# A gated FNet block on one core: one matrix of y's second stage made in chunk 1, then one weight per chunk; two first y units in a row; x of the third block added by accumulating DMA

## The chip, the core and the metric

The kernel runs on one core of a Trainium2 chip. The metric is the device time of one execution in microseconds. For the kernel before there are three timed executions (685.96, 687.7 and 689.08 us, median 687.7) and one profiled execution (683.77 us).

The engines named below: PE (TensorE) multiplies matrices, DVE (VectorE) adds and multiplies element by element, ACT (ScalarE) copies, scales and applies functions, POOL (GpSimd) here only issues DMAs, SP (SyncE) issues most of the DMAs.

## The reference

```python
def _A_ref(x, dft_seq_re, dft_seq_im, dft_hid_re, dft_hid_im):
    a = jnp.einsum("bsd,ed->bse", x, dft_hid_re)
    b = jnp.einsum("bsd,ed->bse", x, dft_hid_im)
    y = jnp.einsum("ts,bse->bte", dft_seq_re, a) - jnp.einsum("ts,bse->bte", dft_seq_im, b)
    return y

def _B_ref(x, w1, b1, w2, b2):
    h = jnp.einsum("bsd,df->bsf", x, w1) + b1
    zero = jnp.zeros_like(h)
    r = jnp.where(h > zero, h, zero)
    h = r * r
    out = jnp.einsum("bsf,fd->bsd", h, w2) + b2
    return out

x = A_x                                # [1, 2048, 512], fp32
xn = _layernorm(x, axis=-1)
s = _A_ref(xn, ...)                    # the DFT over hidden and sequence, real part
g = _silu(_B_ref(xn, ...))             # D = 512, F = 1792
return x + s * g
```

## The kernel before

**Numbers.** All matrix products are fp32 products made of three passes over operands split in two: a high part HI, rounded to the fast type by ACT (`split_hi`, line 130), and the remainder LO, subtracted by DVE (`split_lo`, line 133). `split` makes both, so DVE's half waits for ACT's. Most products of 2x2 blocks are done with seven block products instead of eight (`PRODUCTS`, numbers 1 to 7). Each needs sums of blocks of its operands ahead of the split, on DVE: three instructions per operand, 128x512, 128x256 and 128x256 (`sums_b`, lines 273 to 275, and `sums_a`, lines 279 to 285). The sums of the results are on DVE too (`combine`, line 322, in the chunks; lines 731 and 734 in the units).

**Stages.** The program is one long order written out by hand: the order of the Python calls is the order of the instructions on each engine, and each engine works its own list from front to back.

1. *Chunks* (to about 335 us). The sequence DFT, applied first, in eight chunks of 256 columns over the layer-normalised tokens. Chunks 0 and 1 use eight products with moving operands of 512 columns (`one_product`, line 356). Chunks 2 to 7 use seven products (`mm`, line 341), in eight steps j = 0 to 7 each; a step is 7 x 6 = 42 matmuls of 256 columns. Step n's operand `g` comes from a tile `u` that SP loads four steps ahead (`step_load`), that DVE sums two steps ahead (`step_sums`) and that ACT and DVE split one step ahead (`step_split`). At the end of a chunk the seven results are combined by eight operations: three at the end of the chunk's last step, four behind step 0 of the next, one behind step 1, which then stores the chunk (`PQD`).
2. *The weights beside it.* Between the steps, weights of later stages are prepared by generators, which `go(name)` carries on by one piece: `d0` to `d3` are the hidden DFT's four matrices (the second stage of y), `v0`, `v1`, `v6` three of the seven slices of w1. Each has four pieces (`weight`): a load, the three sums, and two splits (128x768 and 128x1024), each with a store of the result to DRAM. `y0` to `y2` prepare the first operands of the y stage (load, sums, two splits), `p0` to `p3` load the `d` matrices back, half a matrix a piece. The table `EARLY` says which piece runs behind which step (chunk, j) of chunks 2 to 7; `d0` and `d1` are made in chunks 0 and 1 by other means.
3. *y units* (to about 391 us). Eight units `YUnit`, each seven products of 12 matmuls of 256 columns (`products`, line 721). The products of a unit collect in four regions: A (products 1, 2), B (6, 5, 3), C (4), D (7). A is copied, negated, into B by ACT as its start value (`seed`, line 140), B into C likewise. DVE makes C22 from B (line 731) after product 5, and C21 from C (line 734) after product 4; ACT copies A, B and D out, and stores the unit (line 760). Unit 0 runs its products in a row (1, 7, 6, 2, 5, 4, 3). From unit 1 on, the units overlap: a unit's first product runs ahead of the last three of the unit before. The operands of a unit are two tiles `yraw` (load, sums, split).
4. *H units* (to about 543 us). 28 units `HUnit` for the first matrix of the FFN (7 slices of F by 4 blocks of 512 tokens), pipelined in the same way, their outputs stored to DRAM. `H_SIDE` says which pieces of other work run in three places of each unit: `V2` to `V5` make the remaining slices of w1, `w0` to `w6` the slices of w2, `x` the tokens, `h` the operands of the last stage.
5. *Output* (to the end). Four blocks of 512 tokens by seven slices, `outer`, line 827, matmuls into `m_o` (blocks 1 to 3) and `m_last` (block 4); operands `hr` are loaded, summed and split ahead (`h` pieces, and the table `O_SIDE`). A block is finished while the next one runs: `finish` applies silu on ACT, multiplies by y (`times`, line 877, DVE) and adds x. It adds x either by DVE (`plus`, line 882, which then stores on SP) or by a DMA that POOL issues and that adds into the tile in SBUF (`add_x`, line 865), in which case a later `put` (line 868) stores on SP. How many tiles `load_fin` loads decides which: with four all parts are added by DVE, with three the first two by DVE and the others by DMA. Before, it loads three for the first two blocks and four for the third (`c > NTC - 3`).

Of the kernel before, what the change touches and what calls it, by code (L numbers as in the profile page):

```python
# [35 lines left out]


EARLY = {
# [7 lines left out]
}  # L46
# [13 lines left out]

H_SIDE = {
    0: ((), ("V2", "x2"), ("x3",)),
    1: (("V4",), ("V3",), ("V5", "k6")),
    2: ((), ("V4", "V5"), ("k6",)),
    3: ((), ("V5",), ("w4",)),
    4: ((), ("x2", "x3", "m2"), ("x4",)),
# [16 lines left out]
    23: ((), ("h1",), ("w3",)),  # L83
    24: ((), ("w1", "w2"), ("w6", "h2")),
    25: ((), ("w2", "w3"), ("h3", "l4")),
    26: ((), ("w3", "w6"), ("l5",)),
    27: ((), ("h2",), ()),
}
ACT_PAIR = (7, 10, 13, 15, 17, 18, 19, 20, 26)
O_SIDE = {0: (("h4",), ("h5",)), 1: ((), ("w6",))}  # L90

EPS = 1e-5
HI, LO = 0, 1
# [31 lines left out]
def fnet_gated_kernel(ctx, tc, x, xt, ct, wd, w1, w2, b1, b2, out):  # L125
# [41 lines left out]
    def operand_buf(tag, name, step, shape=(2, 7, 256)):  # L167

        first = START.get(tag, 0)
        skip = (step - first) % 4 * LANE  # L170
        size = shape[0] * shape[1] * shape[2]
        room = ROOM.get(tag, 0)
        flat = buf(tag, [P, size + (room or skip)], name, F32R)
        a, b, c = shape
        return flat[:, skip:skip + size].rearrange("p (a b c) -> p a b c", a=a, b=b, c=c)
# [234 lines left out]
        if n < 2 * NC:  # L410
            sums_rows(yraw[n], yraw[n][:, 4:8], True)

    def y_split(n):
        if n < 2 * NC:
            g = yop[n] = operand_buf(Y_HOME[n // 2 % 3][n % 2], f"yg{n}", 1)
            split(g[:, HI], g[:, LO], yraw[n][:, 0:7])

    def y_early(n):

# [109 lines left out]
    for k in range(2):  # L529
        nc.sync.dma_start(PQD[0][:, k].rearrange("p k n -> p (k n)"), plain[k])  # L530
    for j in range(NJ - 1):
        split(*plain_parts(1, j + 1))
        load_c(*order[NJ + j + 4])
        if j == 1:
            go("d0", "d1")
        for h in range(2):
            products(1, j, h)
        beside(split_s1(j - 1) if j else 0)
    step_sums(0)
    step_split(0)  # L540
    step_load(3)
    split_s1(NJ - 2)
# [296 lines left out]
    def load_fin(c):  # L839

        if c < NTC - 1:
            ts = [buf(f"pq{n // 2}{n % 2}", [P, 2, 512], f"fin{c}_{n}") for n in range(4 if c > NTC - 3 else 3)]
        else:
            t = buf("xc5", [P, 3, 2, 512], f"fin{c}")
            ts = [t[:, n] for n in range(3)] + [buf("pq10", [P, 2, 512], f"fin{c}_3")]
        fin[c] = ts
        for n, t in enumerate(ts):
            src = (Y[c], x[c * TC:(c + 1) * TC])[n // 2]
            for i in range(2):
                nc.sync.dma_start(t[:, i].rearrange("p (k e) -> p k e", k=2), at(src, 2 * (n % 2) + i))  # L850
# [32 lines left out]
        nc.sync.dma_start(at(out[c * TC:(c + 1) * TC], k)[:, cols], z.rearrange("p (k e) -> p k e", e=256))  # L883

    go("m0")
    unit = YUnit(0)
    some(closing, 5)
    nc.sync.dma_start(PQD[NC - 1].rearrange("p h k n -> p (h k n)"), e)
    unit.products(1)
    unit.seed("B", "A")  # L890
    y_sums(3)
    unit.products(7)
    unit.m7()
    unit.products(6)
    unit.seed("C", "B")
    y_split(3)
    y_load(6)
    unit.products(2)
    unit.c11()
    unit.products(5)  # L900
    unit.c22()
    unit.products(4)
    unit.c21()
    unit.products(3)
    unit.c12()
    y_sums(4)
    y_sums(5)
    before = None
    for u in range(1, NC):
        n = 2 * u + 2  # L910
        unit = YUnit(u)
        y_split(n)
        y_load(n + 3)
        unit.products(1)
        unit.seed("B", "A")
        if before:
            before.c11()
            before.products(5)
            before.c22()
# [73 lines left out]
    for n in range(NTC * NP):  # L993
        c, p = divmod(n, NP)
        last = c == NTC - 1
        if n and not last and p == 0:

            ms = Banks(c)
            for k in (2, 4, 5):
                bias(ms[k], k)  # L1000
        elif last and p == 0:

            ms = {k: bank(t, f"m{k}_last") for k, t in
                  {1: "b20", 2: "b21", 6: "b30", 7: "b31", 5: "bb", 3: "ba"}.items()}
# [12 lines left out]

        go(*O_SIDE.get(n, ((), ()))[0])
        if n == 1:
            for k, i in ((1, 1), (2, 1), (6, 1), (4, 1), (5, 0), (3, 0), (7, 1), (5, 1), (3, 1)):  # L1020
                add(k, i)
        elif n and (not last or p < REST):
            for k in ORDER if p else FIRST_LAST if last else FIRST:
                add(k, p)
        if n == 1:

            nc.scalar.activation(stats[:, 0, 0, 0:1], stats[:, 0, 0, 0:1], AF.Silu)
        if not n:
            go("h2")
        go(f"h{n + 3}")  # L1030
        if p == NP - 1 and not last:
            e = buf("e", [P, 4, 512], f"z{c}")
            list(combine(lambda k: halves(e[:, k]), ms))
            done_next = c, e
        if c and not last and p in (3, 4):
            put(*done, p - 1)
        go(*[f"h{n + 2}"][:n], *O_SIDE.get(n, ((), ()))[1], f"h{n + 6}")
        if p == (3 if last else 5):
            load_fin(c)
        if p == NP - 1 and not last:  # L1040
            done = done_next
        elif c:
            for k in ((2, 3), (0,), (1,), (), (), (), ())[p] if not last else ((), (0,), (1,), (2,), (3,), (), ())[p]:
                finish(*done, k)


    e = buf("u", [P, 4, 512], f"z{c}")
# [88 lines left out]
```

## Time and profile before

| | us |
|---|---|
| timed runs, median (lowest, highest) | 687.7 (685.96, 689.08) |
| the profiled execution, its own time | 683.77 |
| its span (first to last event of the profile) | 682.0 |
| busy in it: PE | 672.8 |
| DVE | 605.2 |
| ACT | 357.4 |
| POOL | 6.4 |
| mean granted TensorE clock | 0.998 |

How to read the rows below. A row of groups names the line, the engine, the operation, out<-in with the tiles' names, the shape, the count, then busy time and mean. In the timeline a row begins with start and busy time in us, and in brackets stands the engine's idle time before it and what released it. In the chain of waits (what ended last, followed back), a row is start, time, engine, tile and line, with the count of instructions in a row. In the windows, the columns are the window, its length, then the busy time of PE (with the count), of PE's weight loads, the granted clock, the share of DMA and its GB/s. A matmul's end is modelled, so PE's rows can touch although PE loses a little between them.

### The profile page before, as it was taken

What the parts mean: (1) busy time and instruction counts of PE and PEld (TensorE: products, weight loads), DVE (VectorE), ACT (ScalarE), POOL (GpSimd) and SP (SyncE); (2) the same over time, 40 slices, a digit from 0 to 9 for tenths busy, and PEclk for the clock granted to TensorE, in tenths of its full rate; (3) what the DMA queues carried; (4) which work ended last, traced back from release to release, by engine and by line L of the source; (5) the groups of instructions that cost most, each with busy time, mean ns of one, the idle gap of its engine ahead of it and who ended that gap; (6) DMA issues with size and microseconds to landing.
All of it is one profiled execution on the core that took longest, in us unless ns stands there. A gap on an engine that the chain in (4) does not pass through costs nothing.

```text
span 682.0 us, 13144 instructions
## 1 busy us (share of the span) xinstructions
PE 672.8 (99%) x5440; PEld 648.9 (95%) x5440; DVE 605.2 (89%) x849; ACT 357.4 (52%) x475; POOL 6.4 (1%) x9
## 2 busy tenths in 40 slices
PE   9999999999999999999999999999999999999996
PEld 6778789999999999999999999999999999999996
DVE  7999969999999898798899979999847879999996
ACT  4445645444444343435364557787878765454451
POOL 0000000000000000000000000000000000101000
PEclk9999999999999999999999999999999999999999
DMA  8625656758587764349468657679445956777745
GB/s 295 212 93 216 209 232 220 270 182 289 177 281 260 265 231 159 120 162 361 155 234 287 223 186 276 215 283 325 154 155 181 373 191 212 187 218 200 241 147 171
DMA packets 51723, 150.82 MB, mean 221 GB/s; under 512 B 4944, under 2 KB 19536, under 8 KB 50256
## 3 DMA queue, kind: packets, MB, share of 16 engines
q1 hardware_dynamic: 44096, 129.80, 55.8%
q10 hardware_dynamic: 6208, 18.88, 7.0%
q0 software_dynamic: 1360, 1.31, 1.5%
q8 instruction: 42, 0.69, 0.4%
q14 instruction: 17, 0.14, 0.1%
HBM read 101.98 MB, written 47.99 MB: 220 GB/s over the span
## 4 chain that ended last, share of the span: by engine, by line
PE 75%; DVE 18%; issue 3%; ACT 2%; DMA 1%; ACTq 0%; DVEq 0%
PE m L341 22%; PE m_o L827 14%; PE r_B L721 12%; PE pq_b L356 8%; PE r_A L721 8%; DVE g L133 5%; PE r_C L721 4%; PE r_D L721 3%; DVE c L322 3%; PE pq_ba L356 2%; PE pq_bb L356 1%; PE pq_bc L356 1%; ACT g L130 1%; DMA u<-in_ct 1%; DVE u L273 1%
## 5 line engine op out<-in xcount | busy, mean ns | idle before, releaser
L341 PE MATMUL m<-g,xc 128*128 128x256 f32 x2016 | 231.7, 277 | 1.3 <-DVE g L133 1.0
L341 PEld LDWEIGHTS m<-g,xc 128*128 128x128 f32 x2016 | 230.7, 188 | 2.3 <-DVE g L133 2.3
L130 ACT ACTIVATE g<-u 128x1792 fp32r<-128x1792 f32 (+3 forms) x70 | 100.0, 1428 | 139.9 <-PE m L341 91.1
L133 DVE TENSOR_TENSOR g<-u,g 128x1792 fp32r<-128x1792 f32 (+3 forms) x70 | 117.5, 1679 | 19.1 <-ACT g L130 18.8
L827 PE MATMUL m_o<-w,g 128*128 128x256 f32 x882 | 100.5, 276 | 0.0
L827 PEld LDWEIGHTS m_o<-w,g 128*128 128x128 f32 x882 | 100.3, 188 | 0.0
L130 ACT ACTIVATE g<-hr 128x1792 fp32r<-128x1792 f32 (+2 forms) x31 | 48.2, 1565 | 43.0 <-DVE hr L285 17.7
L721 PE MATMUL r_B<-xT,w 128*128 128x256 f32 x504 | 67.6, 277 | 0.3 <-DVE h L791 0.2
L356 PE MATMUL pq_b<-g,xc 128*128 128x512 f32 x240 | 66.2, 394 | 0.3 <-ACT xc L130 0.2
L721 PEld LDWEIGHTS r_B<-xT,w 128*128 128x128 f32 x504 | 61.8, 188 | 1.1 <-DVE h L791 0.7
L133 DVE TENSOR_TENSOR g<-hr,g 128x1792 fp32r<-128x1792 f32 (+2 forms) x31 | 56.7, 1839 | 5.1 <-ACT g L130 5.1
L356 PEld LDWEIGHTS pq_b<-g,xc 128*128 128x128 f32 x240 | 43.7, 188 | 13.0 <-ACT xc L130 3.0
L721 PE MATMUL r_A<-xT,w 128*128 128x256 f32 x336 | 42.9, 276 | 0.0
L721 PEld LDWEIGHTS r_A<-xT,w 128*128 128x128 f32 x336 | 40.3, 188 | 0.0
L721 PE MATMUL r_B<-wdp,yg 128*128 128x256 f32 x288 | 36.0, 278 | 0.9 <-DVE y L731 0.7
L721 PEld LDWEIGHTS r_B<-wdp,yg 128*128 128x128 f32 x288 | 34.1, 188 | 1.4 <-DVE y L731 0.9
L273 DVE TENSOR_TENSOR u<-u 128x512 f32<-128x512 f32 x48 | 32.9, 685 | 2.1 <-DMA u<-in_ct 2.1
L827 PE MATMUL m_last<-w,g 128*128 128x256 f32 x294 | 33.8, 277 | 0.4 <-DVE g L133 0.4
L827 PEld LDWEIGHTS m_last<-w,g 128*128 128x128 f32 x294 | 33.5, 188 | 0.6 <-DVE g L133 0.6
L133 DVE TENSOR_TENSOR yg<-yraw,yg 128x1792 fp32r<-128x1792 f32 x13 | 26.2, 2022 | 3.0 <-ACT yg L130 2.9
L322 DVE TENSOR_TENSOR c<-m,c 128x512 f32<-128x512 f32 x42 | 27.2, 685 | 1.6 <-PE m L341 0.8
L130 ACT ACTIVATE yg<-yraw 128x1792 fp32r<-128x1792 f32 x13 | 22.2, 1708 | 7.7 <-DVE yraw L282 5.9
(180 smaller groups left out, 856.1 us busy)
## 6 DMA issues: line engine op xcount, KB each, us to landing
u<-in_ct SPq DMA_DIRECT2D x63, 512.0 KB, 3.7
hd<-h ACTq DMA_DIRECT2D x28, 512.0 KB, 4.7
hr<-hd SPq DMA_DIRECT2D x28, 512.0 KB, 3.8
wdp<-wdd SPq DMA_DIRECT2D x8, 896.0 KB, 7.2
yraw<-pqd SPq DMA_DIRECT2D x13, 512.0 KB, 5.1
pqd<-c SPq DMA_DIRECT2D x6, 1024.0 KB, 4.4
w<-w1d SPq DMA_DIRECT2D x6, 896.0 KB, 8.7
y<-y ACTq DMA_DIRECT2D x8, 512.0 KB, 4.6
```

Source lines behind the costliest of these rows:

```text
L130: nc.scalar.activation(hi, src, AF.Copy)
L133: nc.vector.tensor_tensor(lo, src, hi.bitcast(F32), op=ALU.subtract)
L273: nc.vector.tensor_tensor(t[:, 0:2], r[:, 0:1].to_broadcast([P, 2, 256]), r[:, 1:3], op=ALU.add)
L322: nc.vector.tensor_tensor(part_(to), m, part_(frm), op=op)
L341: nc.tensor.matmul(ps[:, d], w[:, a_, d * P:(d + 1) * P], halves(mv(b_)), start=first and d == 0 and (a_, b_) == (HI, HI), stop=last and ( ...
L356: nc.tensor.matmul(accs[c][k], w, part[c, j][:, b_, 2 * h:2 * h + 2], start=j == 0 and h == 0 and (a_, b_) == (HI, HI), stop=j == NJ - 1 a ...
L721: nc.tensor.matmul(self.region(REGION[k]), w, mv, start=i == 0 and k in (1, 7), stop=i == len(ops) - 1, skip_group_check=True)
L827: nc.tensor.matmul(m[:, i * 256:(i + 1) * 256], ready[n][:, a_, H_SLOT[a], i * P:(i + 1) * P], W2[p][:, b_, b], start=p == 0 and i == 0 an ...
```

## The change

It has five parts.

- **`EARLY`.** d2's sums and splits move from chunk 2 into chunk 1: its load and its sums at the start of rounds 4 and 6 of chunk 1's loop, its two splits behind the sums of the first operand of chunk 2. Then one weight is made per chunk: d3 in chunk 2, v0 in 3, v1 in 4, v6 in 5, with the load in the last place of the chunk before (d3: the first place of its own), the sums behind step 2 and the two splits behind steps 3 and 4. The y operands y1 and y0 move from chunks 4 and 5 to chunks 5 and 6, and the loads p1 and p0 one behind the other into chunks 5 and 6. Chunk 7's rows stay.
- **The first y units.** Units 0 and 1 run in a row, without overlap; the overlapping loop begins at unit 2. In unit 0 DVE's half of the split of operand 3 stands behind C22.
- **`H_SIDE`, `O_SIDE`.** The second piece of `V4` (its sums) moves within unit 1 from the first place to the second; the second piece of `w6` moves from unit 26 to the first step of the output stage.
- **`load_fin`.** For the third block two tiles (y alone) are loaded in place of four, so x of all its four parts is added by the accumulating DMA, and four `put` follow in the last block.
- `y_split` is given halves so that they can be placed apart.

```diff
 EARLY = {
-    (2, 0): ("d2",), (2, 1): ("d3",),
-    (2, 2): ("d2",), (2, 3): ("d2",), (2, 4): ("d2", "v0"), (2, 5): ("d3",), (2, 6): ("d3",),
-    (3, 2): ("d3", "v1"), (3, 3): ("v0",), (3, 4): ("v0",), (3, 5): ("v0", "v6"), (3, 6): ("v1",),
-    (4, 2): ("v1",), (4, 3): ("v1", "y1"), (4, 4): ("v6",), (4, 5): ("v6",), (4, 6): ("v6", "y0"),
-    (5, 2): ("p1",), (5, 3): ("p1",), (5, 4): ("y0",), (5, 5): ("p0",), (5, 6): ("p0", "y1"),
+    (2, 0): ("d3",), (2, 2): ("d3",), (2, 3): ("d3",), (2, 4): ("d3", "v0"),
+    (3, 2): ("v0",), (3, 3): ("v0",), (3, 4): ("v0", "v1"),
+    (4, 2): ("v1",), (4, 3): ("v1",), (4, 4): ("v1", "v6"),
+    (5, 2): ("v6",), (5, 3): ("v6",), (5, 4): ("v6", "y1"), (5, 5): ("p1",), (5, 6): ("p1",),
+    (6, 2): ("y1", "p0"), (6, 3): ("p0",), (6, 4): ("y0",), (6, 5): ("y0",),
...
-    1: (("V4",), ("V3",), ("V5", "k6")),
+    1: ((), ("V3", "V4"), ("V5", "k6")),
...
-    26: ((), ("w3", "w6"), ("l5",)),
+    26: ((), ("w3",), ("l5",)),
...
-O_SIDE = {0: (("h4",), ("h5",)), 1: ((), ("w6",))}
+O_SIDE = {0: (("h4", "w6"), ("h5",)), 1: ((), ("w6",))}
...
     for j in range(NJ - 1):
+        if j in (NJ - 4, NJ - 2):
+            go("d2")
         split(*plain_parts(1, j + 1))
...
     step_sums(0)
+    go("d2", "d2")
     step_split(0)
...
-            ts = [buf(..., f"fin{c}_{n}") for n in range(4 if c > NTC - 3 else 3)]
+            ts = [buf(..., f"fin{c}_{n}") for n in range(2 if c > NTC - 3 else 3)]
...
-    unit = YUnit(0)
...
     y_sums(3)
+    for u in range(2):
+        unit = YUnit(u)
+        unit.products(1)
+        unit.seed("B", "A")
+        if u:
+            y_split(4)
+            y_load(7)
+        unit.products(7)
+        unit.m7()
+        unit.products(6)
+        unit.seed("C", "B")
+        if u:
+            y_split(5)
+            y_load(8)
+            go(*Y_SIDE[u][0])
+        else:
+            y_split(3, split_hi)
+        unit.products(2)
+        unit.c11()
+        unit.products(5)
+        unit.c22()
+        if not u:
+            y_split(3, split_lo)
+            y_load(6)
+        unit.products(4)
+        unit.c21()
+        unit.products(3)
+        unit.c12()
+        if not u:
+            y_sums(4)
+            y_sums(5)
+    y_sums(6)
+    y_sums(7)
     before = None
-    for u in range(1, NC):
+    for u in range(2, NC):
...
                 finish(*done, k)
+        if last and p in (3, 4, 5, 6):
+            put(*done, p - 3)
```

Three places show how it moves work on DVE. The first is in chunk 4, around the splits of the operands of steps 3 and 4 (`g_3`, `g_4`; `u_5` is a later step's tile, `w11` is v1). Before:

```order
L133 TENSOR_TENSOR g_3_1912<-u_3_1746,g_3_1912 128x1792
L133 TENSOR_TENSOR w11g<-w11r,w11g 128x768
L273 TENSOR_TENSOR u_5_1860<-u_5_1860 128x512
L274 TENSOR_TENSOR u_5_1860<-u_5_1860 128x256
L275 TENSOR_TENSOR u_5_1860<-u_5_1860 128x256
L133 TENSOR_TENSOR g_4_1966<-u_4_1808,g_4_1966 128x1792
L133 TENSOR_TENSOR w11g<-w11t,w11g 128x1024
```

And now:

```order
L133 TENSOR_TENSOR g_3_1906<-u_3_1740,g_3_1906 128x1792
L279 TENSOR_TENSOR w11t<-w11r 128x512
L281 TENSOR_TENSOR w11t<-w11r,w11t 128x256
L282 TENSOR_TENSOR w11t<-w11r,w11t 128x256
L273 TENSOR_TENSOR u_5_1854<-u_5_1854 128x512
L274 TENSOR_TENSOR u_5_1854<-u_5_1854 128x256
L275 TENSOR_TENSOR u_5_1854<-u_5_1854 128x256
L133 TENSOR_TENSOR g_4_1959<-u_4_1802,g_4_1959 128x1792
L133 TENSOR_TENSOR w11g<-w11r,w11g 128x768
```

Between the two operands stood one split of v1; now its three sums stand there, and the splits come one and two steps later. The second place is in the y units 0 and 1, on DVE, from the sums of operand 3 (`yraw_3315`) on; `y_3521` is unit 0's output, `y_3634` unit 1's. Before:

```order
L282 TENSOR_TENSOR yraw_3315<-yraw_3315 128x256
L133 TENSOR_TENSOR yg_3537<-yraw_3315,yg_3537 128x1792
L731 TENSOR_TENSOR y_3521<-r_B,y_3521 128x256
L734 TENSOR_TENSOR y_3521<-r_C,y_3521 128x256
...
L133 TENSOR_TENSOR yg_3601<-yraw_3371,yg_3601 128x1792
L133 TENSOR_TENSOR yg_3621<-yraw_3423,yg_3621 128x1792
```

And now:

```order
L282 TENSOR_TENSOR yraw_3315<-yraw_3315 128x256
L736 TENSOR_TENSOR y_3521<-r_B,y_3521 128x256
L133 TENSOR_TENSOR yg_3537<-yraw_3315,yg_3537 128x1792
L739 TENSOR_TENSOR y_3521<-r_C,y_3521 128x256
...
L133 TENSOR_TENSOR yg_3616<-yraw_3371,yg_3616 128x1792
L133 TENSOR_TENSOR yg_3650<-yraw_3423,yg_3650 128x1792
L736 TENSOR_TENSOR y_3634<-r_B,y_3634 128x256
L739 TENSOR_TENSOR y_3634<-r_C,y_3634 128x256
```

C22 of unit 0 (line 731, now 736) goes ahead of the split, and C22 of unit 1 stands behind both splits of unit 2's operands. The third place is in the last block of the output stage, on DVE, where the operands `g` for the last slices are made from `hr` and the third block `z` is finished. Before:

```order
L133 TENSOR_TENSOR g_7485<-hr_7255,g_7485 128x1792
L877 TENSOR_TENSOR z_7364<-z_7364,fin_0_7307 128x512
L882 TENSOR_TENSOR z_7364<-z_7364,fin_2_7309 128x512
L279 TENSOR_TENSOR hr_7376<-hr_7376 128x512
L284 TENSOR_TENSOR hr_7376<-hr_7376 128x256
L285 TENSOR_TENSOR hr_7376<-hr_7376 128x256
L133 TENSOR_TENSOR g_7537<-hr_7305,g_7537 128x1792
```

And now (the multiplication by y, line 877 before, is line 882 here):

```order
L133 TENSOR_TENSOR g_7479<-hr_7255,g_7479 128x1792
L882 TENSOR_TENSOR z_7358<-z_7358,fin_0_7307 128x512
L279 TENSOR_TENSOR hr_7370<-hr_7370 128x512
L284 TENSOR_TENSOR hr_7370<-hr_7370 128x256
L285 TENSOR_TENSOR hr_7370<-hr_7370 128x256
L133 TENSOR_TENSOR g_7530<-hr_7305,g_7530 128x1792
```

The addition of x is gone from DVE, here and at the three other parts of the block; POOL issues four DMAs (`z_7358<-in_x`) in their place.

More of the change, by code (lines that the diff above doesn't have):

```diff
@@ L411, in y_sums, with y_split @@
             sums_rows(yraw[n], yraw[n][:, 4:8], True)
[L413 to L416, printed above, removed]
+    def y_split(n, *halves_):
+        for half in halves_ or (split_hi, split_lo):
+            if n < 2 * NC:
+                if n not in yop:
+                    yop[n] = operand_buf(Y_HOME[n // 2 % 3][n % 2], f"yg{n}", 1)
+                half(yop[n][:, HI], yop[n][:, LO], yraw[n][:, 0:7])
     def y_early(n):
@@ L841, in load_fin @@
         if c < NTC - 1:
-            ts = [buf(f"pq{n // 2}{n % 2}", [P, 2, 512], f"fin{c}_{n}") for n in range(4 if c > NTC - 3 else 3)]
+            ts = [buf(f"pq{n // 2}{n % 2}", [P, 2, 512], f"fin{c}_{n}") for n in range(2 if c > NTC - 3 else 3)]
         else:
@@ L885, in fnet_gated_kernel @@
     go("m0")
-    unit = YUnit(0)
     some(closing, 5)
     nc.sync.dma_start(PQD[NC - 1].rearrange("p h k n -> p (h k n)"), e)
-    unit.products(1)
-    unit.seed("B", "A")
     y_sums(3)
[L892 to L907, printed above, removed]
+    for u in range(2):
[31 more added lines that the diff above has]
+    y_sums(7)
     before = None
-    for u in range(1, NC):
+    for u in range(2, NC):
         n = 2 * u + 2
```

## The prediction

> **What bounds the kernel now.** I read the engine totals first, then the waits of TensorE (PE), then its timeline and that of VectorE (DVE) around each wait.
>
> ```profile
> PE 672.8 (99%) x5440; PEld 648.9 (95%) x5440; DVE 605.2 (89%) x849; ACT 357.4 (52%) x475; POOL 6.4 (1%) x9
> 354.65 2.72 PE r_A L721 x24
> 61.37 2.04 PE pq_b L356 x9
> 7.73 0.73 PE L356 MATMUL pq_b<-g,xc 128*128 128x512 f32 x2
> 666.17 10.94 PE L827 MATMUL m_last<-w,g 128*128 128x256 f32 x94 [0.39 <-DVE g L133]
> ```
>
> PE is busy throughout, and the change leaves its 5440 matmuls as they are. The two rows of the chain of waits give the pace when nothing is late: 2.72/24 = 0.1133 us for a matmul of 256 columns, 2.04/9 = 0.227 for 512. There are 5040 of the first kind and 384 of the second: 571.2 + 87.0 = 658.2 us. The first product starts at 7.73 and the last ends at 666.17 + 10.94 = 677.11, which is 669.4. So about 11 us (1.6%) is all that can be won between them. It sits in short waits (the wait view's largest row after the start, then the timeline and chain of PE):
>
> ```profile
> PE m L341 <- DVE g L133: 1.0, 2, 0.6
> 141.39 8.78 PE L341 MATMUL m<-g,xc 128*128 128x256 f32 x75 [0.60 <-DVE g L133]
> 180.16 50.02 PE L341 MATMUL m<-g,xc 128*128 128x256 f32 x434 [0.41 <-DVE g L133]
> 218.64 68.10 PE m L341 x587
> 296.47 30.11 PE m L341 x263
> 228.00:258.00 30.00, 30.00 (x256) 29.99 (x256) 1.00 0.64 229
> 258.50:296.00 37.50, 37.50 (x333) 37.50 (x333) 1.00 0.40 141
> ```
>
> Such rows understate a loss, since a matmul's modelled end covers part of a gap; I therefore measure from one resumption to the next. A step of chunks 2 to 7 is 42 matmuls, 4.76 us, and a chunk 38.08. From 141.39 to 180.16 is 38.77 (0.69 lost), to 218.64 is 38.48 (0.40), to 296.47, two chunks, 77.83 (1.67). The last two rows (windows of L341) show a second kind of loss: at a granted clock of 1.00 in both, 256 matmuls in 30 us against 333 in 37.5, a pace of 0.117 against 0.113 us. PE has a slow pace, 4% longer, that sets in at some short waits and lasts until a later one; here from 228 to 258 it cost about 1.2 us.
>
> **Chunks 2 to 7.** Why there is a loss at every chunk border:
>
> ```profile
> 288.54 2.03 DVE L133 TENSOR_TENSOR g<-u,g 128x1792 fp32r<-128x1792 f32 x1 [1.21 <-ACT g L130]
> 290.48 4.00 DVE L322 TENSOR_TENSOR c<-m,c 128x512 f32<-128x512 f32 x6
> 294.40 2.01 DVE L133 TENSOR_TENSOR g<-u,g 128x1792 fp32r<-128x1792 f32 x1
> 305.79 0.68 DVE L273 TENSOR_TENSOR u<-u 128x512 f32<-128x512 f32 x1
> ...
> 125.53 6.39 DMA u<-in_ct
> ```
>
> DVE makes step 0's operand, six sums of `combine`, then step 1's operand, ending at 296.41; PE resumes 0.06 later. DVE was idle ahead of it, so this 0.40 is in the order, and the change leaves it. Chunk 4's 0.69 is above it because two weights crowd chunk 3; with one I count 0.40 there, **0.29 won**. In the two chunks up to 296.47 I count 2 x 0.40 for 1.67, **0.87 won**, if the slow pace doesn't start there. Chunk 3's border also waits for a load behind other transfers (the last row, of the chain), whose neighbours on SP are the same in the changed order; 0.
>
> But the order moves a weight's three sums to stand between step 3's operand and step 4's in chunks 3 to 6 (y1's sums in chunk 6). In chunk 4 now:
>
> ```profile
> 189.48 0.95 DVE L133 TENSOR_TENSOR w11g<-w11r,w11g 128x768 fp32r<-128x768 f32 x1
> 190.35 0.69 DVE L273 TENSOR_TENSOR u<-u 128x512 f32<-128x512 f32 x1
> ...
> 191.87 2.02 DVE L133 TENSOR_TENSOR g<-u,g 128x1792 fp32r<-128x1792 f32 x1
> ```
>
> DVE runs nearly without a gap from the border on (in chunk 7 it is free for this place at 305.79, 0.20 before PE's step 3 at 296.47 + 9.52). The split w11g takes 0.87 from start to start, three sums 1.52. With sums in its place step 4's operand is done at 191.87 + 0.65 + 2.02 = 194.54 and reaches PE at 194.60. PE, which resumed at 180.16 and took 0.11 more for the first matmul after its wait, wants it 3 steps later at 194.55: 0.05 late. Such a wait is not in the trace, so I bound it: 0, since 0.05 may vanish, and 0.33, with the 0.28 by which losses exceed the idle shown (below, unit 1). I take the middle, 0.16; in four chunks **0.65 lost**, 0 to 1.3. Whether each also brings the slow pace is a rival.
>
> **Chunk 1.** d2's work (three sums 1.52, splits 0.87 + 1.13) goes into two holes of DVE where it waits for ACT, which waits for PE:
>
> ```profile
> 87.40 1.23 DVE L133 TENSOR_TENSOR g<-u,g 128x1024 fp32r<-128x1024 f32 x1 [3.32 <-ACT g L130]
> 93.53 2.03 DVE L133 TENSOR_TENSOR g<-u,g 128x1792 fp32r<-128x1792 f32 x1 [3.05 <-ACT g L130]
> ```
>
> 3.32 holds 1.52 and 3.05 holds 2.00, so 0. On SP d2's load stands ahead of u_0's, which must wait for a split anyway. If that load is late, ACT's copy of d2 holds up ACT's split for the 87.40 row, and PE wants that operand a product later; without the holes the 3.5 us of DVE work would stand on the path.
>
> **The y units.** Unit 0 now:
>
> ```profile
> 336.39 2.03 DVE L133 TENSOR_TENSOR yg<-yraw,yg 128x1792 fp32r<-128x1792 f32 x1 [1.78 <-ACT yg L130]
> 338.33 0.42 DVE L731 TENSOR_TENSOR y<-r_B,y 128x256 f32<-128x256 f32 x1
> 338.81 1.65 PE L721 MATMUL r_B<-wdp,yg 128*128 128x256 f32 x12 [0.68 <-DVE y L731]
> 341.35 1.71 ACT L130 ACTIVATE yg<-yraw 128x1792 fp32r<-128x1792 f32 x1 [0.47 <-ACT y L140]
> 342.96 0.37 ACT L140 ACTIVATE r_B<-r_A 128x256 f32<-128x256 f32 x1
> 340.29 1.52 PE L721 MATMUL r_A<-wdp,yg 128*128 128x256 f32 x12
> 343.38 1.65 PE L721 MATMUL r_B<-wdp,yg 128*128 128x256 f32 x12 [0.21 <-ACT r_B L140]
> 344.86 2.98 PE L721 MATMUL r_A<-wdp,yg 128*128 128x256 f32 x24
> ```
>
> The sum C22 stands behind a 2 us split, and unit 1's seed behind ACT's split. Products are 12 matmuls, 1.36 us apart. From 340.29 to 344.86 is 4.57 for three of them (4.08): the second wait cost 0.49, 0.28 more than the idle it shows. So the first cost 0.68 + 0.28 = 0.96. Both go: C22 is put ahead of the split, the seed ahead of ACT's split. With units 0 and 1 in a row (what follows are estimates from the durations just quoted, DVE's sums at 1.52 and splits at 1.94), unit 1's products follow from 339.32, its last (into r_B) at 347.48. But its C22 now stands behind both splits of unit 2, and the second can't start on ACT before the seed of C (343.6): ACT to 343.95 + 1.71, DVE to 347.6, C22 at 348.0; 0.7 lost. Unit 2's first split then holds up its seed in the same way (ACT free at 350.6, split to 352.3, seed 352.65 for a product wanted at 352.29): 0.5. The DVE work displaced by these waits reaches unit 2's C22 at 362.8 for 362.3: 0.65. So 1.45 against 1.85: **0.4 lost**, between 1.45 won (nothing new) and 1.6 lost (two more such waits, of 0.6, in unit 3).
>
> **Units H and the last block.**
>
> ```profile
> 412.31 0.68 DVE L279 TENSOR_TENSOR w1raw<-w1raw 128x512 f32<-128x512 f32 x1
> 413.83 0.48 DVE L791 SCALAR_TENSOR_TENSOR h<-r_B,b1s,h 128x256 f32<-128x256 f32 x1
> 414.37 0.97 PE L721 MATMUL r_B<-xT,w 128*128 128x256 f32 x6 [0.18 <-DVE h L791]
> 537.29 0.69 DVE L273 TENSOR_TENSOR w2raw<-w2raw 128x512 f32<-128x512 f32 x1
> 538.82 0.42 DVE L731 TENSOR_TENSOR h<-r_B,h 128x256 f32<-128x256 f32 x1
> 538.30 1.96 PE L721 MATMUL r_B<-xT,w 128*128 128x256 f32 x12
> 540.10 0.87 PE L721 MATMUL r_A<-xT,w 128*128 128x256 f32 x6
> 653.92 0.69 DVE L882 TENSOR_TENSOR z<-z,fin 128x512 f32<-128x512 f32 x1
> 664.10 2.02 DVE L133 TENSOR_TENSOR g<-hr,g 128x1792 fp32r<-128x1792 f32 x1
> z<-in_x POOLq DMA_DIRECT2D x5, 256.0 KB, 4.9
> ```
>
> V4's sums (1.52, behind them C22 at 413.83) move behind unit 1's work on DVE: **0.46 won** (0.18 + 0.28). w6's sums likewise at 537.29: 540.10 - 538.30 less 12 x 0.1133 is **0.44 won**; they move behind the last unit's sums, where PE has the other operands of block 1 at hand. Three of four additions of x (L882, 0.61 from start to start) stood ahead of the operand made at 664.10, for which PE lost 0.39 + 0.28: without them it is 1.8 earlier, **0.67 won**. Each becomes a DMA on POOL (busy 1%), landing 4.9 after its issue; the last is issued near 667, so the four stores, on SP behind the last loads, go out by 673, ahead of those of block 4. SP's queue holds nothing else then that PE needs.
>
> The Trainium skill, "SBUF — State Buffer", box on the "DVE blocks DMA" trap, speaks against this: descriptors of a DMA issued on GpSimd wait while VectorE holds the shared port (about 620 ns alone, 3100 overlapped). By that rule the four would land five times later, an estimate of 24.5 us; by the row above, taken while DVE is busy 89%, they land in 4.9, and I keep the row.
>
> **Sum**, against the profiled execution (span 682.0, own time 683.77, the 1.77 around it unchanged): 0.29 + 0.87 - 0.65 - 0.4 + 0.46 + 0.44 + 0.67 = 1.7 won, so 682.1 for it. The three runs shown had a median of 687.7 (685.96 to 689.08), 3.9 above it: runs differ by more than the sum, probably by how long the slow pace holds. Carried over: 687.7 - 1.7 = **686.0**.
>
> **Rivals.** *Faster:* no new wait appears at step 4 or in units 1 and 2 (0.65 + 1.85 more). For it: these waits are small differences of sums over many rows. Against: the DVE chain they rest on has hardly a gap. 686.0 - 2.5 = 683.5.
>
> *Slower:* the slow pace. Each short wait is a draw: at 228 it set in after one too short for the wait view. The change adds seven short waits, and one that leaves a long stage in the slow pace costs 4% of it: units H from 434 to 533 4.0, the last stage from 545 to 665 4.8, the y units (55 us) 2.1. One of each, last stage and y units: 686.0 + 6.9 = 692.9; slower than before from 1.7 us, that is from 43 us of it. For it: runs shown are 2 to 5 us above the profiled one. Against: in the profile the long stages run at the fast pace, and the change removes waits there.
>
> *Not what it says:* the waits only change place, DVE's total being nearly the same (four additions of 0.69 fewer): 687.7.
>
> *Starved stores:* the four accumulating DMAs are held up by DVE, which works without a pause in the last block. If each of the four had to wait for the end of DVE's work, which is after PE's end at 677.11, the last would land at 677.1 + 4.9 = 682.0 and, with about 4 for its store, end near 686: 4 more than 682.0, so 687.7 + 4 = 691.7, and slower by 4. For it: DVE is busy 89% of the span. Against: the POOL row. By the Trainium skill's factor, with 24.5 for the landing of the last one, issued near 667, the end would be near 695.5.
>
> **How the numbers follow.** Forecast 0.33 and "not what it says" 0.14, faster rival 0.34, slow pace 0.17, starved 0.02. A difference under 0.5%, 3.4 us, can't be told from none here: faster means below 684.3, slower above 691.1. The forecast and the moved waits lie within it, the faster rival beyond it, the slow pace and the starved stores on the other side. So faster 0.34, same 0.47, slower 0.19. Range: down to 682.3 (the faster rival and 1.2 less of the slow pace), up to 690.7 (the y units at their worst, 1.2, and 3.5 of slow pace); the forecast alone 684.4 to 688.5.
>
> **What would show it.** Right: resumptions of PE 38.5 apart at chunk borders, short waits at step 4 of chunks 3 to 6, waits on C22 in y units 1 and 2 and none at unit 0, none on w1raw, w2raw or z. Wrong: a border above 0.5 lost, a stretch over 30 us at 0.117, PE idle before `m_last`, or a store of block 3 that ends last.

## The result

The change made the kernel slower: 693.47 us median (689.77 to 699.55) against 686.38 (685.0 to 689.08), six runs each; the ratio is 1.0102, with a 95% interval of 1.0054 to 1.0150. Measured once more beside its parts it was 1.0098 (1.0070 to 1.0126). The forecast was 686.0, within 682.3 to 690.7.

| | before | after |
|---|---|---|
| profiled execution, own time, us | 683.77 | 689.77 |
| span | 682.0 | 688.0 |
| start of the last matmul | 676.84 | 676.44 |
| from there to the end (called the tail below) | 5.17 | 11.56 |

TensorE (PE) starts its last matmul 0.4 us *earlier*. All of the 6.0 us between the two profiles, and 0.4 more, arise behind it. The windows at the end show this (columns: window, its length, busy time of PE, its weight loads, VectorE (DVE), ACT and POOL, the granted clock, the share of the DMA engines, GB/s), first of before:

```profile
675.00:680.00 5.00, 2.11 (x19) 1.91 (x17) 3.58 (x8) 1.29 (x3) 0.00 (x0) 0.92 0.59 189
680.00:688.00 8.00, 0.00 (x0) 0.00 (x0) 0.00 (x0) 0.00 (x0) 0.00 (x0) 0.75 0.05 16
```

and of after:

```profile
665.00:670.00 5.00, 5.00 (x47) 5.00 (x46) 1.42 (x3) 1.23 (x2) 1.21 (x1) 1.00 0.51 105
670.00:675.00 5.00, 5.00 (x47) 5.00 (x46) 4.83 (x9) 0.63 (x1) 1.22 (x1) 1.00 0.50 105
675.00:680.00 5.00, 1.72 (x16) 1.52 (x14) 3.18 (x7) 1.28 (x3) 1.21 (x1) 0.97 0.69 157
680.00:688.00 8.00, 0.00 (x0) 0.00 (x0) 0.00 (x0) 0.00 (x0) 0.00 (x0) 0.50 0.55 132
```

After 680 no engine computes in either kernel; in after the DMA engines are still busy for 55% of 8 us. What they do stands in the timelines of POOL and SP of after. POOL's last five DMAs, four for the third block and one for the last block's first part, C11:

```profile
654.59 1.21 POOL L870 DMA_DIRECT2D z<-in_x  x1 [29.46 <-DVE z L882]
663.28 1.22 POOL L870 DMA_DIRECT2D z<-in_x  x1 [7.48 <-DVE z L882]
668.10 1.21 POOL L870 DMA_DIRECT2D z<-in_x  x1 [3.59 <-DVE z L1079]
673.11 1.22 POOL L870 DMA_DIRECT2D z<-in_x  x1 [3.80 <-DVE z L1079]
677.76 1.21 POOL L870 DMA_DIRECT2D z<-in_x  x1 [3.43 <-DVE z L882]
```

SP's last stores (line 873 is `put`, line 888 the store of `plus`):

```profile
663.02 14.85 SPq L873 DMA_DIRECT2D out<-z  x4
677.96 0.42 SPq L888 DMA_DIRECT2D out<-z  x1
683.19 0.37 SPq L873 DMA_DIRECT2D out<-z  x1
683.66 1.46 SPq L888 DMA_DIRECT2D out<-z  x3
```

In before, POOL had only C11's DMA at this place, and SP's last stores went six us earlier (POOL's timeline, then SP's; the store on line 883 is that of `plus`):

```profile
671.37 1.21 POOL L865 DMA_DIRECT2D z<-in_x  x1 [46.84 <-DVE z L877]
```

```profile
677.81 1.94 SPq L883 DMA_DIRECT2D out<-z  x3
```

In after, DVE had been ready for POOL's DMAs long before they went. Its multiplications that release the four of the third block, in its timeline:

```profile
653.49 0.69 DVE L882 TENSOR_TENSOR z<-z,fin 128x512 f32<-128x512 f32 x1
...
657.55 0.68 DVE L882 TENSOR_TENSOR z<-z,fin 128x512 f32<-128x512 f32 x1
...
661.61 0.69 DVE L882 TENSOR_TENSOR z<-z,fin 128x512 f32<-128x512 f32 x1
...
664.14 0.69 DVE L882 TENSOR_TENSOR z<-z,fin 128x512 f32<-128x512 f32 x1
```

The second DMA could have gone at 658.2 and went at 663.28, the fourth at 664.8 and went at 673.11. The releaser in brackets is misleading: the DVE instructions named there at 668 and 673 belong to another block. The time of an issue is set by the landing of the DMA before: the first one's store went at 663.02, 0.26 ahead of the second's issue, and from then on the issues are 4.82, 5.01 and 4.65 apart, about one landing (4.9 in the median of the profile's page). So C11's addition, fifth in the line, went at 677.76 in place of 671.37. SP works its list in order: C11's store waited for it until 683.19, and the last three stores, ready by 679, stood behind that store until 683.66. In before they went at 677.81. That is 5.85 of the 6.4 by which the tail grew.

Ahead of the end, matmul by matmul (both kernels have 5440; the start of one in after less its start in before):

| at | after less before, us |
|---|---|
| first matmuls of chunk 2 (99.3) | -0.07 |
| in its step 2 (109.5) | +0.18 |
| end of chunk 7 (332.1) | -0.14 |
| y stage (381.2) | +0.80 |
| H units (420.4) | +0.68 |
| first output block (554.8) | +0.29 |
| last block (669.7) | -0.39 |

The steps behind these figures show in four places of after. The first is the chain of waits in chunk 1, where d2's load took 8.38 us and is on the chain:

```profile
78.12 8.38 DMA wd2r<-in_wd
87.19 0.70 DVE wd2t L273
```

The second is in chunk 6. y0's load is now issued one step (4.76 us) ahead of its sums, where six steps lay between them before. It landed 5.14 us after its issue, DVE waited 0.83 for it, and step 7's operand came 0.45 late, a wait that the prediction did not have (chain, then DVE's and PE's timeline; 0.17 is the idle time shown, 0.45 the gap between the matmuls' starts beyond the pace, over two matmuls). Five of the seven profiles with the whole of `EARLY` show it, with 0.45 to 0.91; in the two others PE ran at its slow pace there.

```profile
276.37 5.14 DMA yr<-pqd
```

```profile
281.53 0.69 DVE L279 TENSOR_TENSOR yt<-yr 128x512 f32<-128x512 f32 x1 [0.83 <-DMA yr<-pqd]
```

```profile
286.65 13.54 PE L341 MATMUL m<-g,xc 128*128 128x256 f32 x117 [0.17 <-DVE g L133]
```

The third is PE's timeline in the y units, with the two waits on C22 where they were forecast (units 1 and 2):

```profile
347.89 1.68 PE L726 MATMUL r_B<-wdp,yg 128*128 128x256 f32 x12 [0.39 <-DVE y L736]
...
363.32 1.65 PE L726 MATMUL r_B<-wdp,yg 128*128 128x256 f32 x12 [0.69 <-DVE y L736]
```

The fourth is DVE's timeline just ahead of the second of these waits, where it waited 0.54 for a tile `yraw` that landed late, which the prediction did not have either:

```profile
359.39 0.69 DVE L279 TENSOR_TENSOR yraw<-yraw 128x512 f32<-128x512 f32 x1 [0.54 <-DMA yraw<-pqd]
```

### The profile page after: what moved, and what is told of

Its sections match the earlier page's. It is cut to its first block, busy times and chain, and to the rows that moved or that the text cites. A ratio compares the mean times of both kernels' runs of the same rounds, so it can differ in the third digit from the quotient of the medians.

```text
span 688.0 us, 13138 instructions
## 1 busy us (share of the span) xinstructions
PE 671.1 (98%) x5440; PEld 647.6 (94%) x5440; DVE 602.0 (88%) x845; ACT 357.5 (52%) x475; POOL 11.3 (2%) x13
## 4 chain that ended last, share of the span: by engine, by line
PE 69%; DVE 19%; DMA 5%; ACT 3%; issue 2%; SPq 0%; DVEq 0%; ACTq 0%
PE m L341 19%; PE m_o L832 15%; PE r_B L726 12%; PE r_A L726 8%; DVE g L133 6%; PE r_C L726 4%; PE r_D L726 4%; PE m_last L832 3%; PE pq_b L356 3%; DVE c L322 2%; DMA u<-in_ct 2%; ACT g L130 1%; PE pq_bc L356 1%; DVE u L273 1%; PE pq_bb L356 1%
## 5 line engine op out<-in xcount | busy, mean ns | idle before, releaser
L341 PE MATMUL m<-g,xc 128*128 128x256 f32 x2016 | 231.3, 277 | 1.6 <-DVE g L133 1.3
L341 PEld LDWEIGHTS m<-g,xc 128*128 128x128 f32 x2016 | 229.8, 188 | 3.1 <-DVE g L133 2.8
```

Of the source, the lines that this page charges most:

```text
L341: nc.tensor.matmul(ps[:, d], w[:, a_, d * P:(d + 1) * P], halves(mv(b_)), start=first and d == 0 and (a_, b_) == (HI, HI), stop=last and ( ...
```

## The experiments

All ratios are to the kernel before, measured beside the run on the same chip. The times in us come from two chips: the kernel before had a median of 686.98 beside the runs with 688.23, 689.55, 687.8 and 690.63 us, and of 684.9 to 685.1 beside all others, so only the ratios compare across these two groups. Three theories are tested: **one at a time** (POOL issues an accumulating DMA only when the one before has landed), **starvation** (DVE's work holds those DMAs up), **short waits** (PE's new waits and its slow pace make the loss).

**The third block's x added by DVE again.** Of the change, `load_fin` goes back to four tiles and the four `put` go.

```diff
-            ... for n in range(2 if c > NTC - 3 else 3)]
+            ... for n in range(4 if c > NTC - 3 else 3)]
-        if last and p in (3, 4, 5, 6):
-            put(*done, p - 3)
```

> The change with its third block finished as before: four tiles loaded, x added by VectorE, no accumulating DMA for it. Theory 'one at a time' (GpSimd issues the next accumulating DMA only when the one before has landed, about 4.9 us each; the five end near 683, and the last stores stand behind them): the tail behind the last matmul falls from 11.6 to 5.2 us and the wait of 0.67 ahead of the last block's operands comes back, so the profile's span goes from 688.0 to about 682.3 and the time from 693.5 to about 687.8. Theory 'VectorE starves the DMA' says the same here. Theory 'short waits' (TensorE's new waits and its slow pace make the loss): 693 to 694.

Measured: 688.23 us, ratio 1.0013 (0.9997 to 1.0030); from the last matmul to the end 5.17 us, as before. The larger part of the loss is in this part of the change, not in PE's waits. (The span of this one profile is 687.8, since PE ended at 682.6 there; see the slow pace below.)

**Four accumulating DMAs in place of five.** The last block's C11 is finished by DVE.

```diff
     times(c, e, C11)
-    add_x(c, e, C11)
+    plus(c, e, C11)
-    put(c, e, C11)
```

> The change with only the last block's first part (C11) finished by VectorE, so that four accumulating DMAs are issued in place of five. One at a time: the four are still issued about 4.9 us apart (654.6, 663.3, 668.1, 673.1), the last lands near 677.9 and its store goes then, with the others directly behind it; span about 682.5 to 683, time about 688. Starvation: the four are late as before and the stores behind them too, but VectorE has 0.69 us more to do near the end; span 683 to 684, so this run tells it apart by the spacing alone. Short waits: span 688, time 693.5.

Measured: 689.55 us, ratio 1.0033 (1.0013 to 1.0054); the tail is 6.3 us. The four were issued at 656.62, 663.85, 668.86 and 673.87, the same spacing. With the fifth out of the line the stores at the end no longer wait for it, though DVE has more to do: the loss arises in POOL's queue.

**More room for descriptors.** The program sets aside a space in SBUF for the descriptors of POOL's DMAs (the entries that say which pieces of data to move), 1024 bytes of a partition in this kernel. This run sets aside twice that. To make room, the second half of b2 is left out: only the first half is loaded, and it stands in for both.

```diff
-    b2s = pool.tile([P, D], F32, name="b2s")
+    b2s = pool.tile([P, 256], F32, name="b2s")
...
-    nc = bacc.Bacc(..., dynamic_dma_scratch_size=1024)
+    nc = bacc.Bacc(..., dynamic_dma_scratch_size=2048)
```

> The change with twice the space for the descriptors of GpSimd's DMAs (2048 bytes of a partition in place of 1024); to make room, only the first half of b2 is kept and used for both halves. If the DMAs go one at a time because this space holds one DMA's descriptors: the five are issued as VectorE gets ready for them (about 654.6, 658.6, 662.7, 665.2, 671), the tail falls to about 5 us, span about 681.7, time about 687. If GpSimd waits for each DMA to land for another reason: spacing 4.9 as before, span 688, time 693.5. Starvation: issues may come earlier but the landings stay where they were, near 663, 668, 673, 678 and 683, span 688. Short waits: 693.5.

Measured: 687.8 us, ratio 1.0010 (0.9994 to 1.0026), tail 5.4 us. POOL's timeline in this run:

```profile
587.68 2.58 POOL L870 DMA_DIRECT2D z<-in_x  x2 [587.24 <-DVE z L882]
620.80 2.46 POOL L870 DMA_DIRECT2D z<-in_x  x2 [30.55 <-DVE z L882]
657.64 1.21 POOL L870 DMA_DIRECT2D z<-in_x  x1 [34.37 <-DVE z L882]
661.70 1.20 POOL L870 DMA_DIRECT2D z<-in_x  x1 [2.85 <-DVE z L882]
665.76 1.20 POOL L870 DMA_DIRECT2D z<-in_x  x1 [2.86 <-DVE z L882]
668.36 1.22 POOL L870 DMA_DIRECT2D z<-in_x  x1 [1.40 <-DMA out<-z]
674.09 1.21 POOL L870 DMA_DIRECT2D z<-in_x  x1 [4.50 <-DVE z L882]
```

The third block's four go 0.4 us behind DVE's multiplications (which end at 657.28, 661.34, 665.40 and 667.94), and the pairs of the first two blocks, which were over 5 us apart, go back to back. Nothing of DVE's work was changed. So it is this space that holds the next DMA back: with 1024 bytes one such DMA is under way at a time, and the next waits until its room is free. Starvation falls with it; in after the spacing was also nearly the same whether DVE was busy 1.42 of 5 us (665 to 670) or 4.83 (670 to 675).

**The same from the other side: halves.** The changed kernel, each addition issued as two DMAs of 128 KB, with 1024 bytes.

```diff
-        nc.gpsimd.dma_start(z, at(x[...], k), accum_op=ALU.add)
+        for i in range(2):
+            nc.gpsimd.dma_start(z[:, i], at(x[...], k)[:, i], accum_op=ALU.add)
```

> The changed kernel with every accumulating DMA issued as two of half the size (128 KB each), with 1024 bytes for the descriptors as before. If this space is what holds the next DMA back, and holds one of full size (17 packets on each of 16 engines) but not two, it holds three of the half size (9 each): the two halves of a part are issued 1.2 us apart, the last block's come earlier than in the changed kernel, the fifth pair before 675, the tail is 5 to 7 us, time 3 to 5 us below the changed kernel (ratio to the kernel before 1.003 to 1.006). If GpSimd waits for each DMA whatever its size: ten in a row of 3 to 4 us each, the last issued after 680, and the time is not below the changed kernel's.

Measured: 687.11 us, ratio 1.0030 (1.0013 to 1.0048), tail 5.4 us. POOL's timeline of the first pairs, and of the start of the last block:

```profile
589.45 2.80 POOL L871 DMA_DIRECT2D z<-in_x  x3 [589.01 <-DVE z L883]
594.29 0.89 POOL L871 DMA_DIRECT2D z<-in_x  x1 [2.04 <-issue]
622.62 2.66 POOL L871 DMA_DIRECT2D z<-in_x  x3 [27.44 <-DVE z L883]
628.43 0.88 POOL L871 DMA_DIRECT2D z<-in_x  x1 [3.15 <-issue]
659.45 1.77 POOL L871 DMA_DIRECT2D z<-in_x  x2 [30.14 <-DVE z L883]
```

Three go back to back, the fourth waits. The queue row of the profile's page, of after and then of this run, gives the packets:

```profile
q0 software_dynamic: 2448, 2.36, 2.4%
```

```profile
q0 software_dynamic: 2592, 2.36, 2.5%
```

That is 272 packets for each of 9 DMAs, 17 for each of 16 DMA engines if they are spread evenly, and 144 for each of 18 halves, 9 for each engine. One of 17 fits but not two (34), three of 9 (27) but not four (36). If the space is filled by packets, an inference from these counts, 1024 bytes have room for 27 to 33 of them for each DMA engine.

**The third block's x alone.** The kernel before with this one part of the change (the reverse of the first run).

> The kernel before with only the third block's x added by accumulating DMA. One at a time, and starvation: TensorE ends 0.7 us earlier, the tail is 6.4 us longer, so span about 687.7 and time about 692. Short waits: the wait of 0.67 ahead of the last block's operands is gone and nothing else changes, span 681.4, time 685.7.

Measured: 690.63 us, ratio 1.0055 (1.0036 to 1.0073), tail 10.5 us, 5.4 longer than before. It loses by itself; 0.68 was won ahead of the last block, as expected.

**The whole change again.**

> The changed kernel once more, beside its parts, since its first six runs give an interval of 1% in all. If the accumulating DMA costs about 4 us (the runs with and without it) and the rest about 1 to 2: ratio 1.007 to 1.010.

Measured: 692.37 us, ratio 1.0098 (1.0070 to 1.0126). Its profile has the same code as after, a span of 692.3 and a tail of 10.3 (11.56 in after); the last matmul started at 681.99 in place of 676.44. Where most of these 5.5 us went is in the windows of L341, of after and then of this run:

```profile
112.00:140.00 28.00, 28.00 (x249) 28.00 (x248) 1.00 0.57 197
235.00:255.00 20.00, 20.00 (x179) 20.00 (x178) 1.00 0.91 327
```

```profile
112.00:140.00 28.00, 28.00 (x241) 28.00 (x240) 1.00 0.60 199
235.00:255.00 20.00, 20.00 (x172) 20.00 (x171) 1.00 0.84 291
```

These are the same matmuls at the same granted clock, without an idle time, and yet 249 against 241 and 179 against 172 in the same time. This is the slow pace. Summed over all matmuls from 97 to 404 us whose spacing is near 117.8 ns instead of 113.35, it lasted 16 us in after and 158 here, and 3.8% of the difference is 5.4. By the same count it lasted 16 to 250 us in the eight profiles with d2 in chunk 1 and 12 to 180 in the six without. So one profile's span cannot be compared with another's to a few us, only the tail, the waits and the medians can.

**EARLY alone**, on the kernel before.

> The kernel before with only the change to the table EARLY and d2 made in chunk 1. By the prediction: short waits of about 0.15 us at step 4 of chunks 3 to 6 and a border less of 0.29, so 0 to 1 us won, ratio 0.999 to 1.000. If the slow pace of TensorE sets in more often with more short waits: 1 to 3 us lost, ratio 1.002 to 1.004.

Measured: 687.87 us, ratio 1.0035 (1.0014 to 1.0055): a loss, against the prediction, of the size that the expectation gave to the slow pace. The next run shows that nearly all of it comes with d2's move.

**d2 alone in chunk 1.** Of EARLY only the move of d2.

```diff
-    (2, 0): ("d2",), (2, 1): ("d3",),
-    (2, 2): ("d2",), (2, 3): ("d2",), (2, 4): ("d2", "v0"), (2, 5): ("d3",), (2, 6): ("d3",),
+    (2, 1): ("d3",),
+    (2, 4): ("v0",), (2, 5): ("d3",), (2, 6): ("d3",),
```

> The kernel before with only d2 made in chunk 1 (its four pieces leave chunk 2, all else of the table stays). If d2's late load and copy in chunk 1 make EARLY's loss (a wait of about 0.6 ahead of chunk 2's first steps, and the slow pace behind it): 1.5 to 2.5 us lost, ratio 1.002 to 1.0035, with the wait near 102 and a slow stretch from 108 to 142 in the profile. If the loss is the new waits at step 4 of chunks 3 to 6 and what they start: ratio 0.999 to 1.001 here.

Measured: 687.63 us, ratio 1.0031 (1.0009 to 1.0053): nearly all of EARLY's loss. ACT's timeline of this run shows what goes late in chunk 1:

```profile
87.10 0.63 ACT L140 ACTIVATE wd2r<-wd2r 128x512 f32<-128x512 f32 x1 [4.88 <-DMA wd2r<-in_wd]
87.64 1.05 ACT L130 ACTIVATE g<-u 128x1024 fp32r<-128x1024 f32 x1
```

and PE's what follows in chunk 2:

```profile
102.48 5.05 PE L341 MATMUL m<-g,xc 128*128 128x256 f32 x42 [0.28 <-DVE g L133]
107.94 4.27 PE L341 MATMUL m<-g,xc 128*128 128x256 f32 x34 [0.40 <-DVE g L133]
```

d2's load lands 8.9 us after its issue (8.2 to 9.2 in all eight profiles with d2 in chunk 1, 5.4 to 5.6 in the six with it in chunk 2). ACT's copy of d2 waits for it with the split of chunk 1's last operand behind; that split started at 86.30 in before and starts at 87.64 here. DVE's later work is late by some 0.8 us (the split that starts at 99.64 in before starts at 100.40), and PE, which ran from 96.98 to 107 without a wait in before, waits at the first step's end too. By the 504th matmul this profile is 0.82 behind before. That much of the loss is traced to the late load. The other part of the 2.7 us in the medians I cannot account for from profiles: in this one a slow stretch follows, from 108 to 182 us (about 2.8 us), but two of six profiles without d2 in chunk 1 have the same stretch, and a third has part of it.

**The y units alone.**

> The kernel before with only y units 0 and 1 in a row. The prediction has 0.4 lost, between 1.45 won and 1.6 lost. By the runs with the whole change, a tile yraw that lands late holds up C22 of unit 2 as well: from where the chunks end to the H units, 1 to 4 us lost against the kernel before, ratio 1.002 to 1.005.

Measured: 685.53 us, ratio 1.0014 (0.9992 to 1.0037): a small loss or none. In the profiles the wait on C22 of unit 2 varied with the landing of `yraw`: a gap of 0.34 in PE's matmuls in this run, 0.97 in after, up to 2.47 in the others with the whole order. In this run's profile the stage loses 0.41, the figure forecast, but by luck: the new waits (0.66, 0.41 and 0.34) cost no more than the old ones saved, and the 0.4 is the slow pace, which held for about 11 us of it.

**V4 and w6 alone.**

> The kernel before with only V4's and w6's sums moved. By the prediction 0.46 and 0.44 won, ratio 0.9987. If V4's sums only hold up another C22 (as a wait of 0.33 in H unit 1 of the whole change suggests), the second alone is won: 0.45, ratio 0.9993.

Measured: 683.39 us, ratio 0.9970 (0.9950 to 0.9990): faster by 0.3%. In its profile PE gains 0.65 at V4's old place, 0.2 of it a slow stretch that is gone, and 0.45 at w6's.

**Two combinations.** The moves of V4 and w6, with the third block's first two parts added by DMA and the other two by DVE:

```diff
-            ts = [buf(...) for n in range(4 if c > NTC - 3 else 3)]
+            ts = {n: buf(...) for n in ((0, 1, 3) if c > NTC - 3 else (0, 1, 2))}
...
-        if len(fin[c]) > 2 + k // 2:
+        if 2 + k // 2 in fin[c]:
...
+        if last and p in (5, 6):
+            put(*done, p - 5)
```

> A combination: the kernel before with V4's and w6's sums moved, and of the third block's x the first two parts added by accumulating DMA (ready early, so that POOL is free again before the last block's part at 671) and the last two by VectorE. TensorE's wait of 0.67 ahead of the last block's operands goes, the tail stays at 5.2: 0.7 below the run with the sums alone, ratio 0.996. If even two DMAs reach into the end: tail over 7, ratio 0.998 to 1.000.

and the same with C22 of y unit 0 and the start value of unit 1 ahead of the splits, the units still overlapped:

```diff
-    y_split(3)
-    y_load(6)
+    y_split(3, split_hi)
     unit.products(2)
     unit.c11()
     unit.products(5)
     unit.c22()
+    y_split(3, split_lo)
+    y_load(6)
...
-        y_split(n)
-        y_load(n + 3)
+        if before:
+            y_split(n)
+            y_load(n + 3)
         unit.products(1)
         unit.seed("B", "A")
+        if not before:
+            y_split(n)
+            y_load(n + 3)
```

> The same with y unit 0's C22 put ahead of VectorE's split and unit 1's start value ahead of ScalarE's split, units overlapped as before. The waits of 0.96 and 0.49 go and no load is delayed: 1.0 to 1.4 below the other combination, ratio 0.994. If the splits, now later, hold up unit 2: no better than the other, ratio 0.996.

Measured: 683.76 us, ratio 0.9975 (0.9955 to 0.9996), and 682.42 us, ratio 0.9969 (0.9954 to 0.9985). Both lie below the kernel before by their intervals; that they beat the two moves alone is not shown. The 0.996 expected of the first lies within its interval, the 0.994 expected of the second below it. In both the wait ahead of the last block's operands is gone and the tail is 5.3 us, so two DMAs that are ready early pass through. In the second the waits on C22 and on the start value are gone, but the list of PE's waits has a new one for unit 2's operand, as the expectation's second case has it:

```profile
PE r_A L723 <- DVE yg L133: 1.0, 1, 1.0
```

## Why the prediction was wrong

**Where it failed.** The step "Each becomes a DMA on POOL ... landing 4.9 after its issue; the last is issued near 667, so the four stores ... go out by 673" took the issue of each at the time its operand is ready, so that the DMAs would overlap. They do not: with this kernel's 1024 bytes one is under way at a time. The fourth went at 673.11, and C11's addition, which the step did not count as queued behind them, 6.4 us late. The sum had put the tail at nothing; it grew by 6.4 in after, 5.2 in the second profile of the same code and 5.4 with this part alone, against which the 0.67 won ahead of the last block (0.68 measured) is small. The profile of before showed it, in a place that was not quoted: the first two blocks have two such DMAs each, both released by one pair of multiplications (DVE's timeline, then POOL's).

```profile
583.28 1.29 DVE L877 TENSOR_TENSOR z<-z,fin 128x512 f32<-128x512 f32 x2
```

```profile
584.28 1.32 POOL L865 DMA_DIRECT2D z<-in_x  x1 [583.83 <-DVE z L877]
589.45 1.23 POOL L865 DMA_DIRECT2D z<-in_x  x1 [3.85 <-DVE z L882]
617.47 1.21 POOL L865 DMA_DIRECT2D z<-in_x  x1 [26.80 <-DVE z L877]
623.30 1.23 POOL L865 DMA_DIRECT2D z<-in_x  x1 [4.62 <-DVE hr L279]
```

Both were ready by 584.57, and the second went at 589.45, one landing after the first. With 4.9 for each, counted from the first at 654.6, the fifth could not go before 674.2 instead of 671.4, and later yet if one lands slowly (the first took 8.4 here, beside the loads of `fin`).

**Chunk 1.** "So 0" failed too. The condition that the prediction named itself, a late load that holds up ACT's copy and the split behind it, came true; d2 alone costs 0.31% (0.09 to 0.53), some 2 us, of which 0.82 is traced to this load and the rest stays open. Loads that land late are a term that the sum put at nothing in three places: d2 here, y0 in chunk 6, `yraw` in the y units.

**Chunks 3 to 6.** The waits at step 4 are there: gaps in PE's starts at 155.4, 194.3, 232.9 and 271.8 in after, each about 0.14 beyond the pace; 0.16 was the middle value taken. The 0.29 for chunk 4's border was not won: that wait lost 0.69 before and 0.67 after. Of the 0.87 up to chunk 7's border, 0.28 shows, net of two of the new waits: chunk 6's border lost 0.62 where 0.40 was counted, and y0's late load brought the wait of 0.45 ahead of step 7, with none left at chunk 7's border.

**The y units.** 0.4 lost was forecast, within 1.45 won and 1.6 lost: 0.94 in after's profile and 0.14% (-0.08 to 0.37) alone. The waits at units 0 and 1 went and the three others came, as said: 0.66, 0.40 and 0.97 for the 0.7, 0.5 and 0.65 forecast. What the sum missed is the late `yraw` tile (in the 0.97) and about 0.4 of slow pace.

**H units and the last block.** w6's 0.44 was 0.45 alone. V4's 0.46 was won alone (0.65), but in the whole change only 0.10 of it shows, since another C22 just ahead waited 0.12 longer (as it did with d2 alone, where V4 had not moved) and the slow pace held from 405 to 422 us. The 0.67 ahead of `m_last` was 0.68.

**The rivals.** "Starved stores" had the right place and the right sign and came nearest in size (691.7, 4 lost of the some 7 measured), but with the wrong mechanism, so that its nearness is luck, and with a chance of 0.02. It was weighed against the landing time of 4.9; the right question was how far apart two issues can be. The Trainium skill's factor of five ("SBUF — State Buffer", section "A bandwidth-pool intuition that's wrong (but worth ruling out)", measured there for a DMA issued on GpSimd beside a `tensor_copy` of VectorE) does not show in this trace: from issue to landing the median is 4.9 us for the nine DMAs of after, as for the five of before. No run here has that `tensor_copy`, so the rule itself is not tested. "Slow pace" is real: 5.4 us between two profiles of the same code. That the change makes it set in more often is not shown. Of the signs named, the short waits at step 4 and those in the y units came, and so did borders above 0.5; the one for this failure, a store of block 3 that ends last, did not, since the last stores were block 4's, behind C11's.

**The sum.** Measured part by part: x of the third block +0.55%, EARLY +0.35%, y units +0.14%, the moved sums -0.30%, together +0.74% against +0.98% to +1.02% for the whole, which the intervals of about 0.2 each leave room for.

## What to carry to other kernels

Before work is moved to a queue, look there for two requests whose operands were ready together, and read how far apart they were issued: this spacing is the price of each further request, while the landing time prices the first alone. Then list what already stands in that queue behind the moved work, and what stands on the storing queue behind the last store that depends on it. Where a load is moved closer to its use, compare the distance with its slowest landing, not with the median. A profiler's named releaser can be an instruction that merely ended at that time.

## What was not expected of the hardware

The space set aside for the descriptors of GpSimd's DMAs limits how many of them are under way: with 1024 bytes one of 256 KB (issues 4.65 to 5.01 us apart) or three of 128 KB (the fourth went once the first had landed), with 2048 bytes at least three of 256 KB (the third went at 665.76, the first one's store at 666.13). And the same program ran the same matmuls, at a granted clock of 1.00, at 113.3 or 117.8 ns each, the slower for stretches of 4 to 119 us, in another pattern in each profile; what starts and ends these stretches beyond a short wait of PE stays open.
